# The second product of a gated MLP by seven block products instead of eight, with single buffers for values, gates and states

## The chip, the cores and the metric

The kernel runs on one core of a Trainium2 chip. The metric is the device time of one execution in microseconds, as the median of several runs. The core has a matrix engine (TensorE, PE in the profile, with its weight loads as PEld), VectorE (DVE), ScalarE (ACT), GpSimd (POOL) and a queue engine (SyncE, SP) that here issues all DMAs. Matrix products are written to PSUM, everything else lies in SBUF.

## The reference

Two blocks follow one another. The first is an mLSTM cell over 768 time steps for 4 batches and 8 heads of width 40:

```python
m_new = np.maximum(f_gate[:, :, t] + m, i_gate[:, :, t])
f_stab = np.exp(f_gate[:, :, t] + m - m_new)
i_stab = np.exp(i_gate[:, :, t] - m_new)
C = f_stab * C + i_stab * outer(vt, kt)
n = f_stab * n + i_stab * kt
y[:, :, t] = sigmoid(o_gate[:, :, t]) * (C @ qt) / np.maximum(np.abs(n @ qt), 1.0)
```

Its output is taken as x, 3072 tokens of width 320, and goes through a small MLP:

```python
h = x @ w_in                                  # 320 -> 2048
g = h * (1.0 / (1.0 + np.exp(-1.702 * h)))
return g @ w_out                              # 2048 -> 320
```

All is f32. The two weight matrices come as pairs of 32-bit words per number (the inputs are 64-bit floats there), which the kernel turns into f32 itself.

## The kernel before

Time is cut into NW = 6 windows of L = 128 steps. Within a window the recurrence is written as matrix products (scores, values, and a state that is carried on), and the 512 tokens of a window (4 batches x 128 steps) go through the MLP together.

A window w has two stages. The **up stage** runs over eight index pairs j (two blocks of 128 hidden columns each): `up` (L366) multiplies xT by w_in for j and j + 1 in PSUM tiles of 512 columns (L376 for two full row blocks, L382 for the last 64 rows), and ACT applies the activation to hidden tiles `gs[w, j]` (L387). Beside it stand, in the first half, `carry` (L341), which takes the window's keys and values into the state, and in the second half `transposes` of the next window's keys and queries (L259; the key copy on ACT, the query copy on VectorE, L266). `gates` (L197) works out the next window's gate sums on VectorE, and `spread` (L268) broadcasts a row of them into the weight tiles by four DMAs.

The **down stage** runs over 16 blocks (batch b, quarter n of the 16 hidden blocks): `down` (L398) multiplies four hidden blocks with w_out in a PSUM tile of 320 columns (L403); after the fourth quarter VectorE copies it out (L407) and SP stores it (L408). After blocks 0, 2, 4, ... 14 one step of the next window's attention is run on the side: first `columns` (L243), then `weights` (L275), `scores` (L295), `values` (L304) and `seam` (L333) for the batches b, one step behind the other. `seam` transposes a batch's result and ACT copies it into xT (L339), which has a single buffer and which the next up stage reads as a whole.

Window 0 is special. The weights are still on their way: `fetch` (L116) loads a piece of raw words and `convert` (L183) turns it into f32 with two ACT and four VectorE operations (L187 to L194). A table `beside` says which pieces are converted and fetched ahead of which block. There are eight pieces of 512 columns of w_in, two for its last 64 rows, and eight of 640 columns of w_out. In window 0 the blocks of the down stage go through half of the hidden blocks for all batches first. Ahead of window 0 a first stage of some 34 us does the attention of window 0, with a few products of zeros (`keep_busy`, L140) between.

The order is written out by hand: each engine runs its instructions in the order of the program, and a framework puts in the semaphores that the tiles need. The hidden tiles and the raw weight pieces share one ring of RING = 10 buffers (`gp`). Values (`v_st`), the state and the o gates have two buffers each; gates f and i of all 768 steps are loaded at once. `ps_a` and `ps_m` have four PSUM tiles each; up and down use `ps_m`.

Of the kernel before, what the change touches and what calls it, by code (L numbers as in the profile page):

```python
# [33 lines left out]
def kernel(  # L34
# [23 lines left out]
    RING = 10  # L58
    assert BH == 32 and D <= DP and DM == 320 and W == 512 and S % L == 0 and NF % 2 == 0
# [5 lines left out]
    gp = ctx.enter_context(tc.tile_pool(name="gp", bufs=RING))  # L65
# [9 lines left out]
    f_sb = const.tile([BH, S], FP, name="f_sb")  # L75
    i_sb = const.tile([BH, S], FP, name="i_sb")
    q_st = const.tile([L, BH, DP], FP, name="q_st")
    k_st = [const.tile([L, BH, DP], FP, name=f"k_st{i}") for i in range(2)]
    v_st = [const.tile([L, BH, D1], FP, name=f"v_st{i}") for i in range(2)]
# [5 lines left out]
    def load(w, part, bs=slice(0, B)):  # L85
        if part and w not in eo:
            eo[w] = ld.tile([L, BH, D], FP, tag="eo", name="eo")
        hs = slice(bs.start * H, bs.stop * H)
        for dst, src in (((v_st[w % 2], v), (eo[w], o_gate)) if part else ((k_st[w % 2], k), (q_st, q))):
            nc.sync.dma_start(out=dst[:, hs, 0:D],  # L90
                              in_=src[bs, :, w * L:(w + 1) * L, :].rearrange("b h s d -> s (b h) d"))
# [5 lines left out]

    def piece_in(c, n):
        return (w_in_sb[:, c, n * 512:(n + 1) * 512].rearrange("p (a b) -> p a b", a=1),
                [(slice(0, 128), w_in_bits[c * 128:(c + 1) * 128, n * 1024:(n + 1) * 1024].unsqueeze(1))])  # L100

    def piece_rest(n):
        return (w_in_x[:, n * 4:n * 4 + 4, :],
                [(slice(i * 64, i * 64 + 64), rest_bits[i][:, n * 4:n * 4 + 4, :]) for i in range(2)])

    def piece_out(f):
        return w_out_sb[:, f:f + 2, :], [(slice(0, 128), out_bits[:, f:f + 2, :])]
# [4 lines left out]
    for n in range(8):  # L112
        pieces += [piece_out(2 * n)]
    bits = {}

    def fetch(n):  # L116
        dst, srcs = pieces[n]
        _, a, b = dst.shape
        bits[n] = gp.tile([128, a, b, 2], U32, tag="g", name="bits")
        for r, src in srcs:  # L120
            nc.sync.dma_start(out=bits[n][r].rearrange("p a b two -> p a (b two)"), in_=src)

    nc.sync.dma_start(out=f_sb, in_=f_gate.rearrange("b h s -> (b h) s"))
    nc.sync.dma_start(out=i_sb, in_=i_gate.rearrange("b h s -> (b h) s"))
    for b in range(B):
        load(0, 0, slice(b, b + 1))
        if b:
            fetch(b - 1)
    for b in range(B):
        load(0, 1, slice(b, b + 1))  # L130
    for n in range(3, RING):
        fetch(n)
# [43 lines left out]
    state = [const.tile([128, BH // 2, 2, D1], FP, name=f"state{i}") for i in range(2)]  # L176
# [3 lines left out]
    kT, qT, wt, ys, xT, gs, o_ps = {}, {}, {}, {}, {}, {}, {}  # L180


    def convert(n):  # L183

        lo, hi, dst = bits[n][:, :, :, 0], bits[n][:, :, :, 1], pieces[n][0]
        dst_u = dst.bitcast(U32)
        A.activation(out=dst, in_=hi.bitcast(FP), func=AF.Abs)  # L187
        A.activation(out=lo, in_=lo, func=AF.Copy, scale=2.0 ** -29)
        V.tensor_scalar(out=dst, in0=dst, scalar1=HI_MIN, scalar2=HI_MAX, op0=OP.max, op1=OP.min)
# [4 lines left out]
        V.tensor_tensor(out=dst_u, in0=dst_u, in1=lo, op=OP.add)  # L194


    def gates(w):  # L197
        c = slice(w * L, (w + 1) * L)
        m = m_at[w]
        f_run = gate.tile([BH, L], FP, name="f_run")  # L200
        m_run = gate.tile([BH, L], FP, name="m_run")
        st = stacked[w] = gate.tile([3 * BH, L], FP, name="st")
        V.tensor_tensor_scan(out=f_run, data0=ones, data1=f_sb[:, c], initial=0.0, op0=OP.mult, op1=OP.add)
        a = st[0:BH, :]
        V.tensor_tensor(out=a, in0=i_sb[:, c], in1=f_run, op=OP.subtract)
        if w == 0:
            room = work.tile([L, H, D1], FP, tag="u", name="room").rearrange("p h d -> p (h d)")
            neg, part = room[0:BH, 0:L], room.bitcast(BF)[0:BH, 2 * L:3 * L]
            V.tensor_tensor(out=neg, in0=f_run, in1=i_sb[:, c], op=OP.subtract)
# [6 lines left out]
        if w == 0:  # L216

            rest = m_run
            for j in range(3):
                part = gate.tile([BH, L], BF, name="part")  # L220
                V.tensor_copy(out=part, in_=rest)
                V.tensor_copy(out=m3[j * BH:(j + 1) * BH, :], in_=part)
                if j < 2:
                    left = gate.tile([BH, L], FP, name="left")
                    V.tensor_tensor(out=left, in0=rest, in1=part, op=OP.subtract)
                    rest = left
# [77 lines left out]
    def values(w, b):  # L304
        hs = slice(b * H, (b + 1) * H)
        po = ps_a.tile([L, H, D1], FP, tag="a", name="p_o")
        for p in range(NP):
            for i in range(2):
                h = 2 * p + i
                T.matmul(po[:, h, :], wt[w, b][:, p, i, :], v_st[w % 2][:, b * H + h, :], start=True, stop=True)  # L310
        u = po
        if w:
            pi = ps_a.tile([L, H, D1], FP, tag="a", name="p_i")
            for p in range(NP):
                T.matmul(pi[:, 2 * p:2 * p + 2, :].rearrange("p a b -> p (a b)"), qT[w, b][:, p, :],  # L315
                         state[w % 2][:, b * NP + p].rearrange("p a b -> p (a b)"), start=True, stop=True)
# [24 lines left out]
    def carry(w, b):  # L341
# [3 lines left out]
        G.tensor_tensor(out=vw, in0=v_st[w % 2][:, hs, :], in1=e, op=OP.mult)  # L345
# [7 lines left out]
        new, old = state[(w + 1) % 2], state[w % 2]  # L353
        if w:
            d = cols[w][:, 3 * BH + b * NP:3 * BH + (b + 1) * NP].unsqueeze(2).to_broadcast([128, NP, 2 * D1])
            G.tensor_tensor(out=new[:, ps].rearrange("p j a b -> p j (a b)"),
                            in0=old[:, ps].rearrange("p j a b -> p j (a b)"), in1=d, op=OP.mult)
        for i in range(2):
            r = slice(i * 64, i * 64 + D)
            if w:  # L360
                V.tensor_tensor(out=new[r, ps, i, :], in0=pc[r, :, i, :], in1=new[r, ps, i, :], op=OP.add)  # L361
            else:
                V.tensor_copy(out=new[r, ps, i, :], in_=pc[r, :, i, :])
# [48 lines left out]

    def attention(w):
# [16 lines left out]
    for i in range(2):  # L430
        G.memset(v_st[i][:, :, D:D1], 1.0)
    G.memset(state[1], 0.0)
# [9 lines left out]
    load(1, 0)  # L442
    load(1, 1)
    columns(0)
    keep_busy(4)
    for b in range(B + 1):
# [7 lines left out]
        if b:  # L454
# [3 lines left out]
    beside = [((3, 4), (10, 11)), ((5, 6, 7), (12, 13)), ((8, 9, 10), (14,)), ((11, 12, 13), (15,)), ((14,), (16,)),  # L458
              ((15,), (17,)), ((), ()), ((), ()), ((16,), ()), ((), ()), ((17,), ())]
# [7 lines left out]
    for w in range(NW):  # L467
        more = w + 1 < NW
        for j in range(NF // 2):
            if j % 2 == 0:  # L470
                if w == 0:
                    weights_in(j // 2)
                up(w, j)
            if more:
                if j == (3 if w == 0 else 0):
                    gates(w + 1)
                if j == 4:
                    spread(w + 1)
# [5 lines left out]
        blocks = [(b, n) for b in range(B) for n in range(NF // 4)]  # L484
        if w == 0:

            blocks = [(b, n) for n0 in range(0, NF // 4, 2) for b in range(B) for n in (n0, n0 + 1)]
        for i, (b, n) in enumerate(blocks):
            if w == 0 and i < 7:
                weights_in(4 + i)  # L490
            if w + 2 < NW and i == (1 if w == 0 else 0):
                load(w + 2, 0)
                load(w + 2, 1)
            down(w, b, n)
            if i % 2 == 0 and side:
                run(side.pop(0))
        for step in side:
            run(step)
# [30 lines left out]
```

## Time and profile before

| | us |
|---|---|
| median of 3 runs | 583.89 |
| lowest, highest | 582.61, 585.11 |
| the profiled execution | 585.45 |
| its span | 583.7 |

The profile is of one execution. Its page gives for each engine the busy time, its share of the span and the number of instructions; a strip of 40 slices, in which a digit is the busy share in tenths (PEclk is the clock that TensorE was granted, in tenths of full speed); the chain of work that ended last; and groups of instructions by line of the kernel, with count, busy time, mean duration and the idle time ahead of them, with what ended it. The timeline gives instructions in order of time, equal ones merged: start, length, engine, line, operation, tiles and count. A busy TensorE is a modelled figure: its instructions overlap one another, so the distance between starts counts, not the duration. All numbers below that are taken from it are of this one execution.

### The profile page before, as it was taken

The numbers are of one execution on the slowest core, as the hardware profiler recorded it, in microseconds if no ns is written. First come the engines' busy times: TensorE is split into PE (matmuls) and PEld (weight loads), VectorE is DVE, ScalarE is ACT, GpSimd is POOL, SyncE is SP. The second block draws the span as 40 slices with busy tenths as digits, with TensorE's granted clock in tenths as the row PEclk, the third lists the DMA queues.
The fourth block names the chain that finished last, engine by engine and source line by source line (L and its number), as shares of the span: only waits on it lengthen the run. The fifth ranks groups of instructions, "written<-read, shape, count | busy, mean of one in ns | idle before, by whom it ended". The sixth has DMA issues, their size and how long they took to land.

```text
span 583.7 us, 7051 instructions
## 1 busy us (share of the span) xinstructions
PE 576.0 (99%) x2802; PEld 369.6 (63%) x2802; DVE 180.2 (31%) x431; ACT 178.7 (31%) x383; POOL 60.5 (10%) x104
## 2 busy tenths in 40 slices
PE   8999999999999999999999999999999999999997
PEld 5845467874457885546787445688554678734575
DVE  5755877342011343111334201143310133300000
ACT  5545567212236101225321123610122622122100
POOL 5011001121001012100112100101210010000000
PEclk9979999999999999999999999999999999999999
DMA  9999729804409001246500340900210000000000
GB/s 176 220 227 213 264 56 162 117 24 157 45 1 147 12 12 62 96 45 74 74 11 12 156 46 0 148 12 12 81 77 1 0 12 12 11 12 0 1 24 22
DMA packets 110000, 41.36 MB, mean 71 GB/s; under 512 B 100016, under 2 KB 104272, under 8 KB 109968
## 3 DMA queue, kind: packets, MB, share of 16 engines
q1 hardware_dynamic: 109968, 40.92, 36.3%
q8 instruction: 22, 0.36, 0.3%
q14 instruction: 10, 0.08, 0.1%
HBM read 36.90 MB, written 4.01 MB: 70 GB/s over the span
## 4 chain that ended last, share of the span: by engine, by line
PE 96%; DVE 2%; ACT 1%; POOL 1%; DMA 0%; issue 0%; SPq 0%; DVEq 0%
PE p_out L403 36%; PE p_h L376 30%; PE p_h L382 8%; PE p_o L310 6%; PE p_s L300 4%; PE p_i L315 3%; PE p_t L264 3%; PE p_c L349 2%; PE p_x L338 1%; DMA i_sb<-in_i_gate_dram 0%; PE p_w L285 0%; DVE y L329 0%; PE p_w L280 0%; PE p_idle L142 0%; PE p_w L284 0%
## 5 line engine op out<-in xcount | busy, mean ns | idle before, releaser
L403 PE MATMUL p_out<-w_out_sb,g 128*128 128x320 f32 x768 | 216.1, 436 | 0.0
L403 PEld LDWEIGHTS p_out<-w_out_sb,g 128*128 128x128 f32 x768 | 142.7, 190 | 57.5 <-issue 0.5
L376 PE MATMUL p_h<-xT,w_in_sb 128*128 128x512 f32 x384 | 178.0, 608 | 0.6 <-ACT xT L339 0.6
L376 PEld LDWEIGHTS p_h<-xT,w_in_sb 128*128 128x128 f32 x384 | 70.8, 193 | 91.8 <-issue 88.5
L387 ACT ACTIVATE g<-p_h 128x512 f32<-128x512 f32 x96 | 54.5, 596 | 175.0 <-PE p_h L382 100.8
L339 ACT COPY xT<-p_x 128x384 f32<-128x384 f32 x24 | 11.5, 479 | 168.2 <-PE p_x L338 154.9
L290 ACT ACTIVATE wt<-wt,cols 128x128 f32<-128x128 f32 x160 | 48.0, 392 | 0.0
L382 PE MATMUL p_h<-xT,w_in_x 64*128 64x512 f32 x192 | 47.7, 615 | 0.0
L407 DVE COPY o_sb<-p_out 128x320 f32<-128x320 f32 x24 | 11.7, 486 | 115.0 <-PE p_out L403 115.0
L310 PEld LDWEIGHTS p_o<-v_st,wt 128*128 128x128 f32 x384 | 45.3, 192 | 1.1
L310 PE MATMUL p_o<-v_st,wt 128*128 128x41 f32 x384 | 45.0, 278 | 0.0
L292 POOL TENSOR_SCALAR_AFFINE_SELECT wt<-wt 128x1024 f32<-128x1024 f32 x20 | 21.9, 1093 | 200.7 <-ACT wt L290 200.7
L319 DVE TENSOR_TENSOR u<-p_i,cols 128x328 f32<-128x328 f32 x20 | 10.0, 500 | 91.7 <-PE p_i L315 91.7
L266 DVE COPY qT<-p_t 128x512 f32<-128x512 f32 x20 | 13.6, 690 | 74.8 <-PE p_t L264 74.8
L302 DVE TENSOR_TENSOR wt<-p_s,wt 128x512 f32<-128x512 f32 x48 | 30.8, 683 | 14.5 <-PE p_s L300 14.5
L382 PEld LDWEIGHTS p_h<-xT,w_in_x 64*128 64x128 f32 x192 | 16.5, 186 | 29.6 <-issue 28.8
L361 DVE TENSOR_TENSOR state<-p_c,state 40x164 f32<-40x164 f32 x32 | 10.4, 326 | 65.4 <-PE p_c L349 64.7
L300 PE MATMUL p_s<-qT,kT 40*128 40x128 f32 x384 | 27.9, 285 | 0.2 <-DVE wt L302 0.2
L300 PEld LDWEIGHTS p_s<-qT,kT 40*128 40x128 f32 x384 | 23.3, 187 | 4.3 <-issue 1.9
L331 POOL COPY y<-y 128x64 f32<-128x64 f32 x24 | 5.8, 243 | 187.2 <-DVE y L329 183.7
L315 PE MATMUL p_i<-state,qT 128*128 128x82 f32 x160 | 22.0, 280 | 0.0
L345 POOL TENSOR_TENSOR vw<-v_st,cols 128x328 f32<-128x328 f32 x20 | 14.7, 737 | 56.3 <-PE p_c L349 56.3
(100 smaller groups left out, 362.5 us busy)
## 6 DMA issues: line engine op xcount, KB each, us to landing
wt<-m_row SPq DMA_DIRECT2D x20, 512.0 KB, 5.8
bits<-in_moe_w_out_dram SPq DMA_DIRECT2D x8, 640.0 KB, 5.7
bits<-in_moe_w_in_dram SPq DMA_DIRECT2D x8, 512.0 KB, 6.4
out_dram<-o_sb SPq DMA_DIRECT2D x24, 160.0 KB, 1.8
k_st<-in_k_dram SPq DMA_DIRECT2D x5, 640.0 KB, 6.5
q_st<-in_q_dram SPq DMA_DIRECT2D x5, 640.0 KB, 6.8
v_st<-in_v_dram SPq DMA_DIRECT2D x5, 640.0 KB, 11.2
eo<-in_o_gate_dram SPq DMA_DIRECT2D x5, 640.0 KB, 10.3
```

The source lines that it names most:

```text
L264: T.transpose(pt[:, p, :], src[:, h:h + 2, :].rearrange("p a b -> p (a b)"), ident)
L290: A.activation(out=x[:, h, :], in_=x[:, h, :], func=AF.Exp, scale=-1.0, bias=cols[w][:, b * H + h:b * H + h + 1])
L292: G.affine_select(out=x, in_=x, compare_op=OP.is_ge, fill=0.0, base=0, pattern=[[0, H], [1, L]], channel_multiplier=-1)
L300: T.matmul(pw[i][:, p, :], kT[w, b][r, p, :], qT[w, b][r, p, :], start=True, stop=True)
L302: V.tensor_tensor(out=wt[w, b][:, :, i, :], in0=pw[i], in1=wt[w, b][:, :, i, :], op=OP.mult)
L310: T.matmul(po[:, h, :], wt[w, b][:, p, i, :], v_st[w % 2][:, b * H + h, :], start=True, stop=True)
L315: T.matmul(pi[:, 2 * p:2 * p + 2, :].rearrange("p a b -> p (a b)"), qT[w, b][:, p, :], state[w % 2][:, b * NP + p].rearrange("p a b -> p ( ...
L345: G.tensor_tensor(out=vw, in0=v_st[w % 2][:, hs, :], in1=e, op=OP.mult)
L376: T.matmul(ph[j][i], w_in_sb[:, c, f * 128:(f + 1) * 128], x[:, c, :], start=(first and c == 0), stop=(not first and c == 1))
L382: T.matmul(ph[j][i], w_in_x[r, j, :], x[r, 2, :], start=first, stop=not first)
L387: A.activation(out=g[:, i, :], in_=ph[j][i], func=AF.Gelu_apprx_sigmoid)
L403: T.matmul(po, gs[w, f // 2][:, f % 2, b * L:(b + 1) * L], w_out_sb[:, f, :], start=(f == 0), stop=(f == NF - 1))
```

## The change

From window 1 on the second product is worked out by Strassen's algorithm in Winograd's form, for two batches at a time (c = 0 for batches 0 and 1, c = 1 for batches 2 and 3). The product of a 2 x 2 block matrix (rows: the two batches; columns: the two halves of the 2048 hidden numbers) with the 2 x 2 blocks of w_out (1024 x 160 each) takes seven block products instead of eight. Each block product is eight f32 matmuls into a PSUM tile of 160 columns.

- `weight_sums` works out three new blocks of w_out (t1, t2, t4) and overwrites a fourth (w01), once, in the up stage of window 1 on VectorE.
- `hidden_sums` works out S1, S2, S4 into new tiles and S3 in place of a hidden block, on VectorE: two operations for each of four j as soon as its second hidden tile is there, and two more ("late") after every second j. Each has 2 x 2 x 128 = 512 numbers a partition, for all four batches.
- `down_fast` lists the seven products of a pair c, each with its evictions: VectorE copies or adds the product into the output tiles of the two batches, with eight operations of 160 columns a pair. The rows of the second batch are stored after the sixth product, those of the first after the seventh.
- The side steps of the attention come after blocks 0, 1, 3, 5, 7, 9, 11 and 13 of the 14.

Window 0 keeps the old products. Values, state, o gates and some gate tiles have one buffer; gates are loaded window by window; the hidden tiles have a ring of eight, four of whose buffers hold pieces 6 to 9 of the raw weights first; the other pieces share a pool of six buffers (`sp`) with the sums. The values of the next window are loaded at j = 4 of the up stage, after `carry` has read the old ones, and its o gates at j = 0. w_out is cut into ten pieces of 512 columns, which end within rows, so that a piece takes two or three DMAs; a piece of w_in's last rows takes eight instead of two.

```diff
-    gp = ctx.enter_context(tc.tile_pool(name="gp", bufs=RING))
+    gp = ctx.enter_context(tc.tile_pool(name="gp", bufs=NH))
+    sp = ctx.enter_context(tc.tile_pool(name="sp", bufs=6))
...
     def fetch(n):
-        dst, srcs = pieces[n]
-        _, a, b = dst.shape
-        bits[n] = gp.tile([128, a, b, 2], U32, tag="g", name="bits")
...
+        pool = gp if 6 <= n < 10 else sp
+        bits[n] = pool.tile([128, 512, 2], U32, tag="g", name="bits")
...
         if w:
-            G.tensor_tensor(out=new[:, ps].rearrange("p j a b -> p j (a b)"),
-                            in0=old[:, ps].rearrange("p j a b -> p j (a b)"), in1=d, op=OP.mult)
+            old = state[:, ps].rearrange("p j a b -> p j (a b)")
+            G.tensor_tensor(out=old, in0=old, in1=d, op=OP.mult)
...
+    def weight_sums():
+        V.tensor_tensor(out=t1, in0=w01, in1=w00, op=OP.subtract)
+        V.tensor_tensor(out=t2, in0=w11, in1=t1, op=OP.subtract)
+        V.tensor_tensor(out=w01, in0=w11, in1=w01, op=OP.subtract)
+        V.tensor_tensor(out=t4, in0=w10, in1=t2, op=OP.subtract)
...
+    def hidden_sums(w, js, late):
+        for j in js:
+            if j % 2 == 0 and not late:
+                for x in (1, 2, 4):
+                    sums[w, x, j // 2] = sp.tile([128, 2, 2, 2, L], FP, tag="g", name="s")
+            s1, s2, s4 = (sums[w, x, j // 2][:, j % 2] for x in (1, 2, 4))
+            a00, a10, a01, a11 = hidden(w, j, 0), hidden(w, j, 1), hidden(w, j + 4, 0), hidden(w, j + 4, 1)
+            if late:
+                V.tensor_tensor(out=a10, in0=a00, in1=a10, op=OP.subtract)
+                V.tensor_tensor(out=s4, in0=a01, in1=s2, op=OP.subtract)
+            else:
+                V.tensor_tensor(out=s1, in0=a10, in1=a11, op=OP.add)
+                V.tensor_tensor(out=s2, in0=s1, in1=a00, op=OP.subtract)
...
+        def product(a, b, *adds):
+            po = ps_m.tile([128, DH], FP, tag="m", name="p_out")
+            for f in range(NH):
+                T.matmul(po, a(f), b[:, f, :], start=(f == 0), stop=(f == NH - 1))
+            for dst, x in adds:
+                if x is None:
+                    V.tensor_copy(out=dst, in_=po)
+                else:
+                    V.tensor_tensor(out=dst, in0=x, in1=po, op=OP.add)
...
+        return [lambda: product(block(0, 0), w00, (o00, None)),
+                lambda: product(total(2), t2, (o01, o00)),
+                lambda: product(block(1, 0), w01, (o10, o01)),
+                lambda: product(total(1), t1, (o11, o10), (o01, o01)),
+                lambda: product(block(0, 1), w10, (o00, o00)),
+                lambda: (product(block(1, 1), t4, (o10, o10)), store(1)),
+                lambda: (product(total(4), w11, (o01, o01)), store(0))]
...
-    beside = [((3, 4), (10, 11)), ((5, 6, 7), (12, 13)), ((8, 9, 10), (14,)), ((11, 12, 13), (15,)), ((14,), (16,)),
-              ((15,), (17,)), ((), ()), ((), ()), ((16,), ()), ((), ()), ((17,), ())]
+    beside = [((3, 4), (10, 11, 12, 13, 14)), ((5, 6, 7), (15,)), ((8, 9, 10), (16,)), ((11, 12, 13), (17, 18, 19)),
+              ((14,), ()), ((15,), ()), ((16,), ()), ((17,), ()), ((18,), ()), ((19,), ())]
...
+            if j == 0 and more:
+                load(w + 1, "o")
+            if w == 1 and j == 1:
+                weight_sums()
...
                 if j == 4:
+                    load(w + 1, "v")
                     spread(w + 1)
...
+            if w and j >= 4:
+                hidden_sums(w, (j - 4,), False)
+                if j % 2:
+                    hidden_sums(w, (j - 5, j - 4), True)
...
+        else:
+            blocks = down_fast(w, 0) + down_fast(w, 1)
+            stops = (0, 1, 3, 5, 7, 9, 11, 13)
+        for i, block in enumerate(blocks):
+            if w == 0 and i < 6:
                 weights_in(4 + i)
...
+            block()
+            if i in stops and side:
                 run(side.pop(0))
```

More of the change, by code (lines that the diff above doesn't have):

```diff
@@ L83, with load_gates, load @@
     w_out_sb = const.tile([128, NF, DM], FP, name="w_out_sb")
-    def load(w, part, bs=slice(0, B)):
-        if part and w not in eo:
-            eo[w] = ld.tile([L, BH, D], FP, tag="eo", name="eo")
+    def load_gates(w):
+        for dst, src in ((f_sb, f_gate), (i_sb, i_gate)):
+            dst[w] = ld.tile([BH, L], FP, tag="fi", bufs=4, name="fi")
+            nc.sync.dma_start(out=dst[w], in_=src[:, :, w * L:(w + 1) * L].rearrange("b h s -> (b h) s"))
+    def load(w, what, bs=slice(0, B)):
         hs = slice(bs.start * H, bs.stop * H)
-        for dst, src in (((v_st[w % 2], v), (eo[w], o_gate)) if part else ((k_st[w % 2], k), (q_st, q))):
+        for c in what:
+            if c == "o" and w not in eo:
+                eo[w] = ld.tile([L, BH, D], FP, tag="eo", bufs=1, name="eo")
+            dst, src = {"k": (k_st[w % 2], k), "q": (q_st, q), "v": (v_st, v), "o": (eo.get(w), o_gate)}[c]
             nc.sync.dma_start(out=dst[:, hs, 0:D],
@@ L111 @@
         pieces += [piece_in(0, n), piece_in(1, n)] + ([piece_rest(n // 2)] if n % 2 == 0 else [])
-    for n in range(8):
-        pieces += [piece_out(2 * n)]
+    for n in range(10):
+        pieces += [piece_out(n)]
     bits = {}
     def fetch(n):
-        dst, srcs = pieces[n]
-        _, a, b = dst.shape
-        bits[n] = gp.tile([128, a, b, 2], U32, tag="g", name="bits")
[L120 to L124, printed above, removed]
+        pool = gp if 6 <= n < 10 else sp
+        bits[n] = pool.tile([128, 512, 2], U32, tag="g", name="bits")
+        for r, c, src in pieces[n][1]:
+            nc.sync.dma_start(out=bits[n][r, c].rearrange("p a two -> p (a two)"), in_=src)
+    load_gates(0)
     for b in range(B):
-        load(0, 0, slice(b, b + 1))
+        load(0, "kq", slice(b, b + 1))
         if b:
@@ L129 @@
     for b in range(B):
-        load(0, 1, slice(b, b + 1))
-    for n in range(3, RING):
+        load(0, "vo", slice(b, b + 1))
+    for n in range(3, 10):
         fetch(n)
@@ new lines, in down_fast, with block, total, store @@
+    def down_fast(w, c):
+        o = [op.tile([128, DM], FP, tag="o", name="o_sb") for _ in range(2)]
+        o00, o01, o10, o11 = (o[i][:, n * DH:(n + 1) * DH] for i in range(2) for n in range(2))
+        def block(two, k):
+            return lambda f: gs[w, k * 4 + f // 2][:, f % 2, (2 * c + two) * L:(2 * c + two + 1) * L]
+        def total(x):
+            return lambda f: sums[w, x, f // 4][:, f // 2 % 2, f % 2, c, :]
+        def product(a, b, *adds):
[7 more added lines that the diff above has]
+                    V.tensor_tensor(out=dst, in0=x, in1=po, op=OP.add)
+        def store(two):
+            b = 2 * c + two
+            nc.sync.dma_start(out=out[b * S + w * L:b * S + (w + 1) * L, :], in_=o[two])
+        return [lambda: product(block(0, 0), w00, (o00, None)),
[5 more added lines that the diff above has]
+                lambda: (product(total(4), w11, (o01, o01)), store(0))]
@@ L429 @@
     G.memset(k_st[1][:, :, D:DP], 0.0)
-    for i in range(2):
-        G.memset(v_st[i][:, :, D:D1], 1.0)
-    G.memset(state[1], 0.0)
+    G.memset(v_st[:, :, D:D1], 1.0)
+    G.memset(state, 0.0)
     for b in range(B + 1):
```

90 lines of the change are left out of this document (47 added, 43 removed).

## The prediction

> **What bounds the kernel now.** I read the page from the top: the busy shares, the clock row, the chain that ended last, then the costliest groups.
>
> ```profile
> span 583.7 us, 7051 instructions
> ...
> PE 576.0 (99%) x2802; PEld 369.6 (63%) x2802; DVE 180.2 (31%) x431; ACT 178.7 (31%) x383; POOL 60.5 (10%) x104
> ...
> PEclk9979999999999999999999999999999999999999
> ...
> PE 96%; DVE 2%; ACT 1%; POOL 1%; DMA 0%; issue 0%; SPq 0%; DVEq 0%
> ...
> L403 PE MATMUL p_out<-w_out_sb,g 128*128 128x320 f32 x768 | 216.1, 436 | 0.0
> ```
>
> TensorE is busy 99% of the span and is 96% of the chain; the clock is full except in one early slice. So the time is a sum of TensorE's instructions, and the second product, L403, is the largest group: 216.1 us. It counts 768 although the code issues 6 windows x 64 matmuls = 384: each f32 matmul runs as two instructions, each with its own weight load. The mean of 436 ns is no price, since it overlaps its neighbours (768 x 436 ns is more than half the span). The price is the distance from start to start, and the timeline has it for several widths:
>
> ```profile
> 170.23 0.19 PEld L376 LDWEIGHTS p_h<-xT,w_in_sb 128*128 128x128 f32 x1 [0.24 <-issue]
> 170.66 0.19 PEld L376 LDWEIGHTS p_h<-xT,w_in_sb 128*128 128x128 f32 x1 [0.24 <-issue]
> ...
> 172.80 0.60 PE L264 MATMUL p_t<-ident,k_st 128*128 128x128 f32 x4
> ...
> 173.24 0.60 PE L264 MATMUL p_t<-ident,q_st 128*128 128x128 f32 x4
> ...
> 174.55 2.32 PE L403 MATMUL p_out<-w_out_sb,g 128*128 128x320 f32 x8
> ...
> 176.71 0.25 PE L245 MATMUL p_cols<-ident,st 96*128 96x96 f32 x1
> ...
> 191.52 1.87 PE L310 MATMUL p_o<-v_st,wt 128*128 128x41 f32 x16
> 193.22 1.10 PE L315 MATMUL p_i<-state,qT 128*128 128x82 f32 x8
> 194.25 1.16 PE L300 MATMUL p_s<-qT,kT 40*128 40x128 f32 x16
> ```
>
> 512 columns: 170.66 - 170.23 = 430 ns. 320 columns: (176.71 - 174.55)/8 = 270 ns. 128 columns: (173.24 - 172.80)/4 = 110 ns. That is a line of 0.833 ns a column plus some 3 ns. Narrow products leave it: 41 columns should take 37 ns but take (193.22 - 191.52)/16 = 106, and 82 columns take (194.25 - 193.22)/8 = 129 at most (the hand-over to the next kind is in it). What holds those is the load of 128 weights, at 106 to 129 ns an instruction. A product of 160 columns lies at 136 ns on the line (110 + 32 x 0.833), above that floor, though not by much.
>
> **The change part by part.** *The product.* A window's 128 instructions at 270 ns (34.56 us) become, for two batch pairs, 2 x 7 products x 8 matmuls x 2 = 224 at 136 ns: 30.46 us. That is 4.1 us a window; window 0 keeps the old form, so 5 x 4.1 = **20.5 us less**. The eighth that the algorithm saves is nearly whole, because the fixed part of an instruction is 3 ns.
>
> *The sums on VectorE.*
>
> ```profile
> L302 DVE TENSOR_TENSOR wt<-p_s,wt 128x512 f32<-128x512 f32 x48 | 30.8, 683 | 14.5 <-PE p_s L300 14.5
> ...
> L205 DVE TENSOR_TENSOR st<-i_sb,f_run 32x128 f32<-32x128 f32 x6 | 1.7, 279 | 0.3
> ...
> L407 DVE COPY o_sb<-p_out 128x320 f32<-128x320 f32 x24 | 11.7, 486 | 115.0 <-PE p_out L403 115.0
> ...
> 173.88 0.69 DVE L266 COPY qT<-p_t 128x512 f32<-128x512 f32 x1 [9.16 <-PE p_t L264]
> ```
>
> Two operands of 512 cost 683 ns and of 128 cost 279, so 1.05 ns an element. A window gets 16 sums of 512 (10.9 us) and 16 evictions of 160 (486 - 160 x 1.05 = 0.32 us each) in place of 4 copies (5.1 for 1.9 us): 14 us more. VectorE is 31% busy, so the total fits; the place matters. Take T = 172.80, the end of an up stage. The program puts the q copy, two sums, the second q copy, two sums, then four late sums on VectorE. Copying starts at T+1.08, and at some 0.65 us each the fourth sum (which completes the tile of the second product) ends near T+5.0 and the last late sums on the hidden tiles near T+6.9, the very last at T+7.5. TensorE does transposes to T+1.75, product 1 (16 x 136 ns = 2.2 us) to T+3.9, columns to T+4.5, and needs the second half of product 2's tile at T+5.6; product 3's last tile at T+8.3. Slack is 0.6 and 1.4 us: I take no wait, with bounds of 0 and 1.5 us in each of four windows. Behind these sums sits the columns copy, which then runs near T+8, against T+4.5 before, right behind the transpose; ACT's exponentials wait for it about 1 us more, and the first scores product that they serve is multiplied 2.9 us ahead of its use. In window 5 there are no transposes and the first sums are done earlier: no wait. The four weight sums (1280 elements, 1.5 us each, 6 us) lie in window 1's up stage beside 9 us of matmuls, before carry evictions that nothing on TensorE needs soon: nothing.
>
> *The seam.* Before, the last side step stood after the fifteenth of 16 blocks; now it stands after the last of 14, directly ahead of the next up stage.
>
> ```profile
> 122.36 0.49 PE L338 MATMUL p_x<-ident,y 128*128 128x128 f32 x3
> ...
> 122.88 0.48 ACT L339 COPY xT<-p_x 128x384 f32<-128x384 f32 x1 [8.09 <-PE p_x L338]
> ...
> 34.55 6.51 PE L376 MATMUL p_h<-xT,w_in_sb 128*128 128x512 f32 x8 [0.57 <-ACT xT L339]
> ```
>
> Three transposes start at 122.36 and take 3 x 110 ns, so TensorE could go on at 122.69; the copy of xT ends at 123.36. All of the up stage's matmuls read that tile, so the next could start near 123.42: 0.73 us lost. The same hand-over exists before at window 0 (34.55), with 0.57 us of idle. Four windows get it: **+2.9 us**. Bounds: 4 x 0.57 and 4 x 1.0.
>
> *Window 0.* The weights of the second product now come as ten pieces of 512 columns, and five of them (14 to 18) are converted ahead of the first scores multiply, where three wider ones were.
>
> ```profile
> 13.27 0.43 DVE L189 TENSOR_SCALAR w_in_sb<-w_in_sb 128x512 f32<-128x512 f32 x1 [1.28 <-ACT w_in_sb L187]
> ...
> 15.03 0.69 DVE L194 CUSTOM_DVE_ANT_0 w_in_sb<-bits,w_in_sb 128x1024 uint16<-128x1024 uint16 x1
> ...
> 82.68 8.88 PE L403 MATMUL p_out<-w_out_sb,g 128*128 128x320 f32 x32
> ...
> 85.29 0.82 DVE L194 CUSTOM_DVE_ANT_0 w_out_sb<-bits,w_out_sb 128x1280 uint16<-128x1280 uint16 x1
> ...
> 88.95 2.44 ACT L290 ACTIVATE wt<-wt,cols 128x128 f32<-128x128 f32 x8
> ...
> 95.18 1.28 DVE L302 TENSOR_TENSOR wt<-p_s,wt 128x512 f32<-128x512 f32 x2
> ...
> 96.99 1.88 PE L310 MATMUL p_o<-v_st,wt 128*128 128x41 f32 x16
> ```
>
> A conversion of 512 takes VectorE 15.72 - 13.27 = 2.45 us. Piece 17 starts behind ACT's exponentials (end 91.39), about 92.1; two conversions bring 97.0 and the multiply (1.28) 98.3, where values wanted it at 96.99: 1.4 us late. Piece 14 is now needed in the second block, four matmul instructions after 82.68, at 83.8; as placed before, its conversion ended at 86.1 (2.3 late), but the three conversions ahead of it are now a fifth narrower, and the hidden tiles no longer wait for their buffers, which lets ACT start on it sooner; it should be done by 83.8 or a little after: I take 0.5 of 0 to 2.3, nearer to cover than to none. **+1.9 us** in all, bounds 0 and 6.
>
> *Single buffers and loads.*
>
> ```profile
> v_st<-in_v_dram SPq DMA_DIRECT2D x5, 640.0 KB, 11.2
> ...
> 64.12 0.37 SPq L121 DMA_DIRECT2D bits<-in_moe_w_out_dram  x1
> ```
>
> The values of the next window are fetched in the middle of the up stage, once the carry's POOL products have read the old ones; on SP the four row broadcasts queue behind. They land in 11.2 us, and their first reader (191.52) is 17 us into the down stage: nothing. The gates come by window, small; the o gates in the up stage, one stage ahead of their use. In window 0 the fetch of piece 16 waits for piece 10's conversion (near 69), and values and broadcasts wait behind it on SP; readers come at 89 to 97, which leaves about 20 us. The pieces now need 28 more DMA issues (24 for 8, 16 for 4): at 0.37 us some 10 us of SP, spread over 90; I take nothing, bounds -1 and +3 for the first 35 us. State in place: its readers on TensorE finish a stage before it is overwritten. The output tiles still number two, and the ninth product's eviction waits for a store issued 2 us before; VectorE then holds, and TensorE has four PSUM tiles (6 us): nothing. At the end a 0.32 us addition replaces a 0.49 us copy: -0.2.
>
> **The sum.** -20.5 + 2.9 + 1.9 - 0.2 = -15.9 us. The profiled execution took 585.45 us (span 583.7 and 1.75 around it), which gives 569.6. The median shown is 583.89, 1.56 lower: **568.0 us**.
>
> **The rivals.** *All waits hidden* (the seam's wait covered, conversions in time): only the product and the end count, -20.7, 563.2 us. For it: TensorE's idle is almost nothing now. Against: the seam's copy has no matmul left to lie beside.
>
> *VectorE late.* If sums run later than I place them, product 2 or 3 waits up to 1.5 us in four windows, and window 0 takes its upper bound of 6: 568.0 + 6 + 4.1 = 578. For it: slack of 0.6 us. Against: the timeline's copies follow each other in less than their mean.
>
> *The clock drops at the seam.*
>
> ```profile
> 31.00:34.50 3.50, 2.11 (x11) 0.89 (x9) 1.80 (x7) 0.96 (x3) 1.52 (x4) 0.84 1.10 260
> 34.50:37.00 2.50, 2.46 (x3) 1.18 (x4) 1.71 (x4) 2.48 (x5) 0.34 (x1) 0.50 1.00 309
> ```
>
> After a stretch with TensorE busy 2.11 of 3.50 us the granted clock was 0.50 (busy is the third number, the clock third from the end); the eight matmuls of 34.55 took 6.51 us where 8 x 430 ns is 3.4. Four such drops cost 4 x 3.1 = 12.4: 580.4 us, no change that can be told. Against: the new gap is 0.73 us between full matmuls. The Trainium skill, page "TensorE: Matmul & The Clock Gate", section "Why this matters for your kernels", asks for no gaps over about 3 us; by it this gap is harmless, and no stretch of this trace has a gap just like it.
>
> *Slower: the weight load shows.* If a 160-column product doesn't cover a load of 128 weights, the load sets the pace.
>
> ```profile
> L310 PEld LDWEIGHTS p_o<-v_st,wt 128*128 128x128 f32 x384 | 45.3, 192 | 1.1
> ```
>
> A load lasts 192 ns from end to end; at that pace 224 x 192 = 43.0 us a window, 8.4 more than now instead of 4.1 less: 568.0 + 5 x 12.5 = 631 us. It decides from 34.56 / 224 = 154 ns on. Against: the same loads follow each other every 106 ns at L310, so they are pipelined. The Trainium skill, the same page, section "What overlaps and what doesn't", says that a weight load overlaps running matmuls only in another row group; by that rule load and product would add up, far above 154 ns. The trace disagrees: L403's 320 columns on all 128 rows leave no room in 270 ns for a load of their own.
>
> **How the numbers follow.** Forecast 0.72; all hidden 0.09; VectorE late 0.10; clock drop 0.05; load shows 0.04. The range reaches from 563 (all hidden) to 577 (most of VectorE late), leaving out about 0.12. A measurement of this kernel can tell about 0.5%, that is 581 us: the first three cases are faster (0.91), the clock drop is within (0.05), the load slower (0.04).
>
> **What would show it.** The new product's line should count 1120 TensorE instructions 136 ns apart; 154 or more makes the prediction wrong in sign. The first up matmul of windows 2 to 5 should wait about 0.6 us for xT. Idle of TensorE before product 2 or 3 for VectorE would show the sums late; a clock under 1.0 after the seam shows the drop. In window 0, values of the next window should wait about 1.4 us for the scores multiply.

## The result and the profile after

| | before | changed |
|---|---|---|
| median of 4 runs, us | 583.86 | 570.67 |
| lowest to highest, us | 582.61 to 585.11 | 568.97 to 570.71 |
| the profiled execution, us (span) | 585.45 (583.7) | 568.97 (567.2) |

The ratio of the times is 0.9767, 95% interval 0.9739 to 0.9795: faster by 13.2 us. The two profiled executions differ by 16.5 us. The prediction didn't foresee the 3.3 us between these two numbers; the experiments deal with them last.

From the page of the changed kernel, the last two lines from its list of groups: its span, the busy shares, the clock strip, then groups by line (count, busy us, mean ns, idle time ahead and what ended it). L471 is the new product, L390 the up stage, L401 its activation.

```profile
span 567.2 us, 8277 instructions
...
PE 557.2 (98%) x3282; PEld 401.7 (71%) x3282; DVE 254.8 (45%) x583; ACT 179.5 (32%) x387; POOL 64.4 (11%) x103
...
PEclk9979999999999999999999999999999999999999
...
L390 PE MATMUL p_h<-xT,w_in_sb 128*128 128x512 f32 x384 | 178.2, 609 | 2.8 <-ACT xT L354 2.8
...
L471 PE MATMUL p_out<-w_out_sb,g 128*128 128x160 f32 x480 | 70.5, 300 | 0.0
...
L471 PE MATMUL p_out<-t,s 128*128 128x160 f32 x320 | 47.9, 303 | 0.0
...
L471 PE MATMUL p_out<-w_out_sb,s 128*128 128x160 f32 x160 | 23.8, 302 | 0.0
L471 PE MATMUL p_out<-t,g 128*128 128x160 f32 x160 | 23.5, 300 | 0.0
```

TensorE is still the bound, and the four groups of L471 count the 1120 instructions that were forecast. VectorE went from 180.2 to 254.8 us of work, 75 us more, and none of it shows in front of L471: its idle time is 0.0. What shows is the seam, 2.8 us in five places ahead of L390, where there was 0.6 in one.

The timeline of the changed kernel at the end of window 1's up stage; T is the start of the transposes, 173.36. L455 and L456 are the early sums, L452 and L453 the late ones, L266 the columns copy.

```profile
173.36 0.60 PE L279 MATMUL p_t<-ident,k_st 128*128 128x128 f32 x4
...
175.11 2.34 PE L471 MATMUL p_out<-w_out_sb,g 128*128 128x160 f32 x16
...
177.28 0.25 PE L260 MATMUL p_cols<-ident,st 96*128 96x96 f32 x1
...
177.69 0.69 DVE L456 TENSOR_TENSOR s<-s,g 128x512 f32<-128x512 f32 x1
177.78 2.44 PE L471 MATMUL p_out<-t,s 128*128 128x160 f32 x16
...
179.50 0.68 DVE L452 TENSOR_TENSOR g<-g 128x512 f32<-128x512 f32 x1
180.06 2.34 PE L471 MATMUL p_out<-w_out_sb,g 128*128 128x160 f32 x16
180.10 0.68 DVE L453 TENSOR_TENSOR s<-g,s 128x512 f32<-128x512 f32 x1
...
180.94 0.18 DVE L266 COPY cols<-p_cols 128x32 f32<-128x32 f32 x1
```

Product 1's 16 instructions start at 175.11 and the columns step at 177.28; product 3 starts 2.28 us after product 2: 136 to 142 ns an instruction. In window 5, where nothing stands between the products, it is 135.8 ns on average from start to start, and 269.2 ns for 320 columns before. The fourth early sum ends at 178.38, T+5.0; the last late sum on a hidden tile at 180.18, T+6.8, while product 3 has just begun with other tiles.

The same timeline at the seam from window 1 to 2:

```profile
222.88 0.49 PE L353 MATMUL p_x<-ident,y 128*128 128x128 f32 x3
...
223.41 0.48 ACT L354 COPY xT<-p_x 128x384 f32<-128x384 f32 x1 [6.88 <-PE p_x L353]
...
223.94 2.41 PE L390 MATMUL p_h<-xT,w_in_sb 128*128 128x512 f32 x5 [0.57 <-ACT xT L354]
```

Three transposes of 0.11 us would have let TensorE go on at 223.21; it went on at 223.94, 0.73 us later.

The lengths of the stages, from the first product of one kind to the first of the next, worked out from the starts in the two traces (us):

| stage | before | changed | difference |
|---|---|---|---|
| first stage | 34.55 | 34.44 | -0.1 |
| up, window 0 | 45.31 | 45.14 | -0.2 |
| down, window 0 | 52.30 | 53.14 | +0.8 |
| up, windows 1 to 5 | 42.4 (5: 35.93) | 42.4 to 42.5 (5: 36.03) | +0.4 in all |
| down, windows 1 to 4 | 52.13 (4: 51.64) | 48.83 (4: 48.35) | -3.3 each |
| down, window 5 | 38.04 | 33.69 | -4.35 |

Window 5 has no seam behind it and shows the product alone: 4.0 us of instructions (128 x 269.2 ns less 224 x 135.8) and 0.3 of the shorter end. Windows 1 to 4 show 4.0 less the seam's 0.73.

### The profile page after: what moved, and what is told of

The parts are those of the page before. It is cut to its first block, busy times and chain, and to the rows that moved or that the text cites. A ratio compares the mean times of both kernels' runs of the same rounds, so it can differ in the third digit from the quotient of the medians.

```text
span 567.2 us, 8277 instructions
## 1 busy us (share of the span) xinstructions
PE 557.2 (98%) x3282; PEld 401.7 (71%) x3282; DVE 254.8 (45%) x583; ACT 179.5 (32%) x387; POOL 64.4 (11%) x103
## 3 DMA queue, kind: packets, MB, share of 16 engines
q1 hardware_dynamic: 111920, 40.92, 35.8%
HBM read 36.90 MB, written 4.01 MB: 72 GB/s over the span
## 4 chain that ended last, share of the span: by engine, by line
PE 88%; SPq 4%; DVE 3%; DMA 2%; ACT 1%; issue 1%; DVEq 0%; ACTq 0%
PE p_h L390 29%; PE p_out L471 28%; PE p_h L396 8%; PE p_o L325 6%; PE p_s L315 4%; PE p_out L417 4%; PE p_i L330 3%; PE p_t L279 3%; PE p_c L364 3%; SPq L137 2%; SPq L97 2%; PE p_x L353 1%; DMA bits<-in_moe_w_out_dram 1%; DVE w_out_sb L211 1%; DVE w_out_sb L209 1%
## 5 line engine op out<-in xcount | busy, mean ns | idle before, releaser
L390 PE MATMUL p_h<-xT,w_in_sb 128*128 128x512 f32 x384 | 178.2, 609 | 2.8 <-ACT xT L354 2.8
L390 PEld LDWEIGHTS p_h<-xT,w_in_sb 128*128 128x128 f32 x384 | 70.4, 192 | 94.5 <-issue 88.0
L401 ACT ACTIVATE g<-p_h 128x512 f32<-128x512 f32 x96 | 54.8, 596 | 147.7 <-PE p_h L396 86.3
L471 PE MATMUL p_out<-w_out_sb,g 128*128 128x160 f32 x480 | 70.5, 300 | 0.0
L471 PEld LDWEIGHTS p_out<-w_out_sb,g 128*128 128x128 f32 x480 | 66.7, 190 | 1.0 <-issue 0.5
L471 PE MATMUL p_out<-t,s 128*128 128x160 f32 x320 | 47.9, 303 | 0.0
L476 DVE TENSOR_TENSOR o_sb<-o_sb,p_out 128x160 f32<-128x160 f32 x70 | 21.4, 317 | 53.8 <-PE p_out L471 53.6
L471 PEld LDWEIGHTS p_out<-t,s 128*128 128x128 f32 x320 | 44.2, 190 | 1.1
L396 PEld LDWEIGHTS p_h<-xT,w_in_x 64*128 64x128 f32 x192 | 16.5, 186 | 29.5 <-issue 28.5
L417 PE MATMUL p_out<-w_out_sb,g 128*128 128x320 f32 x128 | 36.3, 437 | 0.0
L417 PEld LDWEIGHTS p_out<-w_out_sb,g 128*128 128x128 f32 x128 | 23.7, 190 | 9.4
```

The costliest lines, as they stand in the source:

```text
L390: T.matmul(ph[j][i], w_in_sb[:, c, f * 128:(f + 1) * 128], x[:, c, :], start=(first and c == 0), stop=(not first and c == 1))
L396: T.matmul(ph[j][i], w_in_x[r, j, :], x[r, 2, :], start=first, stop=not first)
L401: A.activation(out=g[:, i, :], in_=ph[j][i], func=AF.Gelu_apprx_sigmoid)
L417: T.matmul(po, gs[w, f // 2][:, f % 2, b * L:(b + 1) * L], w_out_sb[:, f, :], start=(f == 0), stop=(f == NF - 1))
L471: T.matmul(po, a(f), b[:, f, :], start=(f == 0), stop=(f == NH - 1))
L476: V.tensor_tensor(out=dst, in0=x, in1=po, op=OP.add)
```

## The experiments

### Narrow products without the block algorithm

```diff
+        for f in range(n * 4, n * 4 + 4):
+            for i, po in enumerate(o_ps[w, b]):
+                T.matmul(po, gs[w, f // 2][:, f % 2, b * L:(b + 1) * L], w_out_sb[:, f, i * 160:i * 160 + 160],
+                         start=(f == 0), stop=(f == NF - 1))
...
-            down(w, b, n)
+            (down_halves if w else down)(w, b, n)
```

> The kernel before, with each 320-column matmul of windows 1 to 5 cut into two of 160 columns: the same sums, twice the weight loads, no block algorithm. If a 160-column product covers its weight load (theory): 256 instructions of 136 ns a window, 34.8 us against 34.5 now, so +0.3 us a window and +1.5 us in all, about 585.4 us. If the load shows (rival), at 154 to 192 ns: 39.4 to 49.2 us a window, +24 to +73 us in all.

585.64 us, ratio to before 1.002 (1.0002 to 1.0038), so +1.2 us. The down stages of windows 1 to 4 went from 52.13 to 52.45 us, +0.32 each. Twice the weight loads cost almost nothing at 160 columns: the rival that the load shows is out.

### 80 columns

```diff
-                T.matmul(po, a(f), b[:, f, :], start=(f == 0), stop=(f == NH - 1))
+                T.matmul(po[:, 0:80], a(f), b[:, f, 0:80], start=(f == 0), stop=(f == NH - 1))
```

> The changed kernel with only the first 80 of each product's 160 columns multiplied, and that half used for both; half of the second product's columns are left out. Theory: the load of 128 weights sets the pace, 112 ns an instruction in place of 136: 1120 x 24 ns = 27 us less, about 543 us. Rival (no floor, 0.833 ns a column plus 3): 70 ns, 74 us less, 496 us.

Both theories missed: 644.64 us (630.92 and 658.36), slower than before. In the timeline of window 1 the instructions are first as the theory has them:

```profile
177.65 2.01 PE L471 MATMUL p_out<-t,s 128*128 128x80 f32 x16
179.50 1.95 PE L471 MATMUL p_out<-w_out_sb,g 128*128 128x80 f32 x16
181.29 1.95 PE L471 MATMUL p_out<-t,s 128*128 128x80 f32 x16
```

(181.29 - 179.50)/16 = 112 ns, the floor of the weight load, where the line has 70. But then the clock fell. First the timeline ahead of the fall, then busy time by stretch: length, busy us of PE, PEld, DVE, ACT and POOL with counts, the granted clock, share of the DMA engines and GB/s.

```profile
188.58 0.41 PE L325 MATMUL p_o<-v_st,wt 128*128 128x41 f32 x2 [0.52 <-DVE wt L317]
189.17 1.76 PE L325 MATMUL p_o<-v_st,wt 128*128 128x41 f32 x14 [0.18 <-DVE wt L317]
```

```profile
184.60:191.40 6.80, 6.10 (x53) 5.83 (x53) 1.87 (x6) 6.71 (x23) 2.18 (x2) 1.00 0.07 24
191.50:249.50 58.00, 57.43 (x270) 52.89 (x269) 18.68 (x60) 4.25 (x12) 5.79 (x10) 0.50 0.10 21
628.00:640.00 12.00, 12.00 (x109) 11.98 (x108) 6.27 (x20) 0.62 (x2) 0.00 (x0) 1.00 0.00 1
```

For 58 us TensorE ran at half clock though the profile calls it busy for 57.4 of them, and windows 2 to 4 show the same for 58 to 61 us each. Both runs lost time in this way: their granted clock is 0.81 and 0.85. The up stages, with 512 columns, brought the clock back each time. The 80-column stream alone did not make it fall: in window 5, where nothing else runs on TensorE (628 to 640), the clock stayed at 1.00. Each of the falls in windows 1 to 4 comes where TensorE waits for the scores multiply amid products of 41 columns (0.52 and 0.18 us in window 1); the products behind it then didn't bring the clock back. That 80 columns are worse than 160 in this kernel is shown; what the clock follows is taken up under "The clock of each run".

### The layout alone

```diff
-            if w == 1 and j == 1:
-                weight_sums()
...
-            blocks = down_fast(w, 0) + down_fast(w, 1)
-            stops = (0, 1, 3, 5, 7, 9, 11, 13)
+            blocks = [(lambda b=b, n=n: down(w, b, n)) for b in range(B) for n in range(NF // 4)]
+            stops = range(0, 16, 2)
```

(`hidden_sums` is left out as well.)

> The changed kernel with the old 320-column product in all windows and without the sums: single buffers, new pieces, later loads alone. Theory: nothing but window 0 changes, +0.7 us against the kernel before (0.83 in its down stage, -0.17 ahead of it), so 584.6 us, and the up and down stages of windows 1 to 5 are as long as before within 0.1 us. Rival (a single buffer makes someone wait): 1 us or more in each window, 589 or more.

586.0 us, ratio 1.0033 (1.0015 to 1.0052): +1.6 us, more than the 0.7 expected. The up and down stages of windows 1 to 5 are within 0.15 us of before (42.40, 52.13, ...): no single buffer makes anyone wait. The excess lies ahead of window 1: the down stage of window 0 took 56.40 us in this profile, 3.3 more than in the changed kernel's. Again by stretch:

```profile
99.10:105.90 6.80, 6.80 (x27) 4.91 (x26) 3.59 (x9) 0.00 (x0) 1.27 (x2) 0.50 0.00 0
```

Half clock for 6.8 us, at a place where before had none.

### The sums doubled

```diff
-                V.tensor_tensor(out=s1, in0=a10, in1=a11, op=OP.add)
-                V.tensor_tensor(out=s2, in0=s1, in1=a00, op=OP.subtract)
+                for _ in range(2):
+                    V.tensor_tensor(out=s1, in0=a10, in1=a11, op=OP.add)
+                    V.tensor_tensor(out=s2, in0=s1, in1=a00, op=OP.subtract)
```

(and the same for `s4`)

> The changed kernel with S1, S2 and S4 worked out twice (24 more VectorE operations of 0.6 us a window, the same results). Theory: the second product waits for VectorE once the slack of 0.6 us at the start of the down stage is used: four more operations ahead of it make 2.4 us, so 1.8 us of wait in windows 1 to 4, less than 0.5 us in window 5, about +7.5 us against the changed kernel (578). Rival (VectorE has room, the sums cost nothing anywhere): +0, 570.7.

585.94 us, ratio to before 1.0029 (1.0006 to 1.0052): twice the expected cost, and the whole gain is gone. In window 1, TensorE's timeline and one line of VectorE's:

```profile
177.80 1.90 PE L473 MATMUL p_out<-t,s 128*128 128x160 f32 x12
181.37 0.81 PE L473 MATMUL p_out<-t,s 128*128 128x160 f32 x4 [1.67 <-DVE s L458]
182.01 2.69 PE L473 MATMUL p_out<-w_out_sb,g 128*128 128x160 f32 x16
184.55 2.34 PE L473 MATMUL p_out<-t,s 128*128 128x160 f32 x16
...
193.20 1.75 PE L325 MATMUL p_o<-v_st,wt 128*128 128x41 f32 x14 [0.18 <-DVE wt L317]
```

```profile
180.62 0.69 DVE L458 TENSOR_TENSOR s<-s,g 128x512 f32<-128x512 f32 x1
```

Twelve instructions of product 2 from 177.80 end near 179.43, and the thirteenth starts at 181.37: 1.9 us late. That is near the 1.8 expected, but by two errors that cancel. The last early sum ends at 181.31, 2.9 us later than in the changed kernel (178.38) and not 2.4; and TensorE needs it only at the thirteenth instruction, near T+6.1, and not at the ninth, T+5.6. So the slack was about 1.0 us, not 0.6. Product 3 and the values then wait a little too, and the stage is 3.0 us longer (51.86 for 48.83) in windows 1 and 2. Window 5 is 0.8 us longer, where less than 0.5 was expected. In windows 3 and 4 (53.47 and 52.45) the clock fell as well, for 3.4 us each:

```profile
381.92 1.75 PE L325 MATMUL p_o<-v_st,wt 128*128 128x41 f32 x14 [0.18 <-DVE wt L317]
...
384.53 1.87 PE L315 MATMUL p_s<-qT,kT 40*128 40x128 f32 x16
386.33 3.35 PE L473 MATMUL p_out<-w_out_sb,s 128*128 128x160 f32 x16
...
466.06 0.83 PE L473 MATMUL p_out<-t,s 128*128 128x160 f32 x4 [2.17 <-DVE s L458]
466.71 4.01 PE L473 MATMUL p_out<-w_out_sb,g 128*128 128x160 f32 x16
```

The products behind 384.8 and behind 466.7 take 3.35 and 4.01 us in place of 2.34. The second drop follows a wait of 2.2 us; the first follows one of only 0.2, among products of 41 columns. So the slack was real, though larger than taken, and past it a wait can cost more than itself.

### The last side step one block earlier

```diff
-            stops = (0, 1, 3, 5, 7, 9, 11, 13)
+            stops = (0, 1, 3, 5, 7, 9, 11, 12)
```

> The changed kernel with the last side step after the thirteenth of 14 blocks in place of the fourteenth; nothing else moves. If the seam's wait is only the copy of xT (prediction), a block beside it hides 0.73 us in windows 1 to 4. But the result that the seam transposes is ready some 2.9 us after its values (VectorE's chain of 2.5 and POOL's copy), and only one block of 2.2 us would then lie between, so I expect the wait to move ahead of the transposes: 0 to 0.2 us gained a window, the down stages 48.6 to 48.9 us. Rival (the chain is covered): 48.1 us, 2.9 us less in all.

569.63 us, ratio to before 0.9737 (0.9693 to 0.9781); down stages 48.91 us: nothing gained, as expected. The wait changed its name:

```profile
220.67 0.49 DVE L344 SCALAR_TENSOR_TENSOR y<-eo,den 128x320 f32<-128x320 f32 x1
...
221.30 0.61 PE L353 MATMUL p_x<-ident,y 128*128 128x128 f32 x3 [0.53 <-DVE y L344]
```

### All side steps one block earlier

```diff
+            if w and more and j == 7:
+                side = attention(w + 1)
+                run(side.pop(0))
             if w and j >= 4:
...
-            stops = (0, 1, 3, 5, 7, 9, 11, 13)
+            stops = (0, 2, 4, 6, 8, 10, 12)
```

> The changed kernel with the columns step of windows 2 to 5 ahead of the last sums, at the end of the up stage, and all other side steps after blocks 0, 2, 4, ... 12, so that two blocks lie between any two and one behind the seam. Theory: the down stages of windows 1 to 4 go from 48.83 to 48.10 us (0.73 each, 2.9 in all), and the columns copy no longer waits behind the sums. Rival (the first scores wait, since VectorE is late with the sums): 48.8 us or more, and TensorE shows idle time before its values for VectorE.

565.92 us, ratio 0.9688 (0.9666 to 0.9709). The seam's wait is down from 2.8 us in five places to 0.6 in one, window 0's:

```profile
PE p_h L390 <- ACT xT L354: 0.6, 1, 0.6
PE p_o L325 <- DVE wt L317: 0.6, 2, 0.3
```

(from the list of waits: total us, times, longest.) The down stages took 47.60 us, the up stages 42.89 with the columns step in them: 0.84 us less for the pair, 3.4 us in all. Starting the columns copy ahead of the late sums (177.20, T+3.6, in place of T+7.6) gave the attention the time that the shorter spacing took; the two moves weren't tried apart.

### Window 0's conversions later

```diff
-              ((14,), ()), ((15,), ()), ((16,), ()), ((17,), ()), ((18,), ()), ((19,), ())]
+              ((14,), ()), ((15,), ()), ((16,), ()), ((), ()), ((), ()), ((17,), ()), ((18,), ()), ((19,), ())]
...
-            if w == 0 and i < 6:
+            if w == 0 and i < 8:
```

> The changed kernel with pieces 17, 18 and 19 converted ahead of blocks 5, 6 and 7 of window 0 in place of 3, 4 and 5, behind the first scores multiply. Theory: TensorE's wait of 0.6 us for that multiply goes, the down stage of window 0 returns from 53.14 to the 52.30 us of the kernel before, about 0.8 us less. Rival (the wait moves to the second half's first block, which then lacks its weights): 53 us or more.

566.62 us, ratio 0.9692 (0.9666 to 0.9719). The stage took 52.13 us, 1.0 less. Yet the median fell by 4.1 us against the changed kernel's 570.67. The rest goes with the clock: three of the five runs are at 0.997 to 1.0, where the changed kernel's four are at 0.991 to 0.994, while the profiled run, at 0.993, is only 1.1 us faster than the changed kernel's profiled run.

### Both repairs

> The last two together: 0.8 + 2.9 = 3.7 us less than the changed kernel if they add up, span near 563.5 us where the early stage runs as in the changed kernel's profile. Rival (one covers the other): 3 us or less.

563.24 us, ratio 0.9627 (0.9604 to 0.9651). By stages the two add up: 3.4 + 1.0 us. The span of 559.9 us is 7.2 below the changed kernel's; the 2.8 us left lie ahead of window 0's down stage, where this profile has no fall of the clock.

### The clock of each run

Every run comes with its mean granted clock, and it sorts the times. Before, 45 runs: 582.4 to 584.1 us at 0.999 to 1.0 (21 runs), 585.3 to 587.3 at 0.995 or less (13 runs), the rest between, at 0.996 and 0.997. (A span of 570 us with 6.8 us at half clock has a mean of 0.994, with 3.4 us 0.997.) The changed kernel, the layout alone and the two experiments on the seam have one thing in common: TensorE waits 0.6 us in window 0 for the first scores multiply, in two parts of 0.3, amid narrow matmuls. In the profile of "all side steps one block earlier", by timeline and by stretch:

```profile
93.99 0.42 PE L325 MATMUL p_o<-v_st,wt 128*128 128x41 f32 x2 [0.29 <-DVE wt L317]
94.68 1.73 PE L325 MATMUL p_o<-v_st,wt 128*128 128x41 f32 x14 [0.27 <-DVE wt L317]
...
93.30:96.70 3.40, 2.83 (x22) 2.35 (x21) 3.19 (x7) 0.97 (x4) 0.00 (x0) 1.00 0.00 0
96.70:103.50 6.80, 6.80 (x29) 5.19 (x29) 3.78 (x10) 0.00 (x0) 1.27 (x2) 0.50 0.00 0
```

After 3.4 us with TensorE busy 2.83, and most of that on 41 columns, came 6.8 us at half clock. Three kernels ran side by side to test whether the wait is the cause.

> The changed kernel once more, beside the next two on one chip. Theory: the wait of 0.6 us in window 0, amid narrow matmuls, lets the clock drop for 6.8 us at about 97 us in most runs that did not drop at 33, so nearly every run shows a granted clock of 0.991 to 0.995 and 569 to 571 us. Rival (drops fall by chance as in the kernel before): a third to a half of the runs at 0.999 to 1.0 and about 566 us.

569.21 us (567.84 to 570.74), ratio 0.9743 (0.9718 to 0.9768): five of six runs at 0.994, one at 0.997, none higher. Its profile dropped at 35 us, for 3.4 us, and not at 97, although the wait is there.

```diff
+            if w == 0 and i == 6:
+                fill = ps_a.tile([128, W], FP, tag="a", name="p_fill")
+                for _ in range(3):
+                    T.matmul(fill, idle, idle.unsqueeze(1).to_broadcast([128, 4, 128]), start=True, stop=True)
```

> The changed kernel with three products of zeros (0.2 us each) on TensorE ahead of the values step in window 0, in the place of its wait; the scores multiply comes as late as before. Theory (the idle time drops the clock): the stage is no shorter by itself (53.1 us) but the drop at 97 us is gone, runs at 0.996 to 1.0 appear, median about 567. Rival (the drop has another cause, or only the late multiply costs): clock and time as in the changed kernel, 570.7.

567.65 us, ratio 0.9713 (0.9686 to 0.974). The stage is as long as before the filling (53.14 us), but four of six runs are at 1.0 and two at 0.994.

```diff
         if b:
+            if b == B:
+                keep_busy(4)
             seam(0, b - 1)
+    keep_busy(2)
```

> The kernel with both repairs (steps one block earlier, window 0's conversions later) and six more products of zeros in the first stage, in the two waits ahead of window 0's up stage. Theory: the drop at 33 us goes as well, all runs at 1.0, 561.6 us with a scatter under 1 us. Rival (the drop at 33 comes from the low activity of the whole first stage): some runs at 0.993 to 0.997 stay, 563 us.

561.66 us (561.55 to 563.25), ratio **0.9618 (0.9592 to 0.9644)**, the lowest of all versions, though not told apart from both repairs alone; all six runs at 1.0. Two of them are at 563.2, so the scatter is 1.7 us and not under 1: something is left in the start. The same step divides the runs of other kernels at equal clock: of the kernel before ten took 582.4 to 582.8 us and eleven 583.8 to 584.1, all at 0.999 to 1.0, and the changed kernel took 568.97 and 570.7, both at 0.994. In two profiles, this one (563.25) and that of the layout alone (588.01), the full clock was granted only 10 us after the start, and the first stage took 35.8 and 36.0 us; in all others it came after 4 to 6 us, and the stage took 34.1 to 34.6. That the late grant is the step in the other runs too is likely, not shown, since their start isn't recorded.

Taken together: of 29 runs of kernels with the unfilled wait 27 are at 0.995 or less; of 45 runs of the kernel before 13 are, of the 10 with the conversions moved two, of the 6 with the wait filled two. (The runs with doubled sums and with 80 columns are left out, since their clock fell in other places too.) At 0.997 or less, so with the falls of 3.4 us, it is 28 of 29, 24 of 45, 5 of 10 and 2 of 6. So with the wait nearly every run dropped, where about half did before. The changed first stage isn't the cause, since the kernels with the conversions moved and with the wait filled have it too. Where in an unprofiled run the drop fell is not known: of the profiles with the wait four have it at 33 to 35 us, two at 97 to 99, and that of 80 columns has both.

Idle time alone doesn't decide, as a stretch of the changed kernel's profile shows beside that of "all side steps one block earlier" above:

```profile
97.70 1.73 PE L325 MATMUL p_o<-v_st,wt 128*128 128x41 f32 x14 [0.27 <-DVE wt L317]
...
94.40:97.81 3.41, 2.83 (x13) 1.76 (x11) 3.27 (x5) 2.85 (x9) 0.58 (x1) 1.00 0.17 23
97.81:101.22 3.41, 3.41 (x38) 3.33 (x38) 2.68 (x6) 0.00 (x0) 0.00 (x0) 1.00 0.00 0
```

TensorE is busy 2.83 us here too, with the same wait, and the clock stays; but most of this stretch is 320 columns.

In all 13 traces the clock changes only at multiples of 3.41 us from its first full grant. Cut each trace there, up to its last product, and estimate for each stretch the share of time in which columns stream (0.833 ns for each f32 column from the start of its product, half that for the zeros in bf16, twice as long at half clock): the 17 stretches ahead of a fall have 0.27 to 0.38, and none of the 2051 others at full clock has less than 0.395. At half clock it stayed up to 0.84 and came back from 0.90 on. Products of 41 columns every 112 ns stream for 0.31 of the time, of 80 columns for 0.60, of 160 for 0.98. So a wait counts by what it takes from a stretch that is narrow already. This fits every fall in the traces, but it was found in them afterwards, and no run was made to test it.

## Why the prediction was right, and where it was off

**The product**: 20.5 us expected; 224 instructions at 136 ns show in window 5 as 4.0 us, so 20.1 in all. Right to 0.1 us a window, since the distance between starts had been read off wider and narrower products, not the mean duration.

**The sums**: no wait was expected, and L471's idle time is 0.0. The times worked out (T+5.0 and T+6.9) are those of the trace (T+5.0 and T+6.8), and doubling the sums made TensorE wait in product 2, as the theory has it. The slack was about 1.0 us and not 0.6: the first need of the last sum had been put four instructions too early.

**The seam**: 0.73 us expected, 0.73 found, four times, and taken back by moving the steps.

**Window 0**: +1.9 us was taken; the stage grew by 0.8. The wait of values for the scores multiply was there, 0.6 us in the idle column and 0.9 from start to start instead of 1.4, and the wait for piece 14 wasn't. This term was mis-sized, as the timeline shows:

```profile
82.23 8.88 PE L417 MATMUL p_out<-w_out_sb,g 128*128 128x320 f32 x32
82.29 0.69 DVE L211 CUSTOM_DVE_ANT_0 w_out_sb<-bits,w_out_sb 128x1024 uint16<-128x1024 uint16 x1
...
86.74 2.44 ACT L305 ACTIVATE wt<-wt,cols 128x128 f32<-128x128 f32 x8
...
90.81 0.41 DVE L206 TENSOR_SCALAR w_out_sb<-w_out_sb 128x512 f32<-128x512 f32 x1
...
96.27 1.28 DVE L317 TENSOR_TENSOR wt<-p_s,wt 128x512 f32<-128x512 f32 x2
97.01 0.41 PE L325 MATMUL p_o<-v_st,wt 128*128 128x41 f32 x2 [0.30 <-DVE wt L317]
```

Piece 14 was done at 82.98, in time, and with it ACT came to the exponentials 2.2 us sooner than before (86.74 for 88.95). I had left their end where it was; piece 17 started at 90.81, not 92.1, and the multiply at 96.27, not 97.0.

**Buffers and loads**: nothing, and nothing was found in windows 1 to 5. **The end**: -0.2, found -0.3.

**The up stages** of windows 2 to 5 came out 0.1 us longer each, which the sum doesn't have; with the last side step one block earlier they are as before.

So 569.6 us was forecast for an execution like the profiled one, and the profiled one took 568.97: the window 0 term, 1.1 us too long, is partly offset by the product and the up stages, each 0.4 us the other way. The step that failed is the last: "The median shown is 583.89, 1.56 lower: **568.0 us**". That carried the spread of the kernel before over to the changed one. The profile of before was one of the runs whose clock had dropped (0.993), and the median, by its time, was not (583.8 to 584.1 us goes with 1.0). All four runs of the changed kernel dropped, the profiled one too, so its median has no drop to lose. It lies 1.7 us above its profile at the same clock of 0.994, which is likely the step of the start. The rival "the clock drops at the seam" named the mechanism but the wrong place: after the seam's 0.73 us, between wide products, no profile of a kernel at full width shows a drop, while 0.6 us amid narrow ones was enough in two. The Trainium skill, page "TensorE: Matmul & The Clock Gate", section "Why this matters for your kernels", asks for no gaps over about 3 us; the runs here disagree, since with all side steps one block earlier the clock fell at 96.7 us behind two gaps of 0.3.

## What to carry to other kernels

Price a matmul by the distance between starts, at its own width, and find the width at which the weight load takes over: down to 160 f32 columns an algorithm that trades products for additions keeps its eighth, at 80 it would not. Additions on an engine that has room cost nothing only as long as the first one needed is early; work out the clock time of that one sum, and move small urgent operations (here the columns copy) ahead of the bulk. When a change leaves a short wait on TensorE among narrow products, compare the granted clock of many runs, not of one profile, before carrying a difference between profile and median from one kernel to another.

## What the runs showed of the hardware

The half clock came in stretches of 3.4 or 6.8 us in the kernels of full width. It fell only behind stretches of 3.41 us in which columns streamed for 0.38 of the time or less (an estimate from the starts in the 13 traces), with 0.2 to 0.9 us of idle time among products of 41 columns as one way to get there. A stream of 80-column products, 112 ns each, ran at 1.00 in window 5 and stayed at half clock for 58 us where the clock had fallen already. Among 160-column products 2.17 us of idle time brought the fall once, and 1.67 us three times didn't. Filling the gap with products of zeros was enough to lower its rate, without saving any of the wait itself.
